# Attention and two mixtures of experts on one core: another order of the first blocks, later splits for the third unit, and other counts of idle products

## The chip, the core and the metric

The kernel runs on one core of a Trainium2 chip. A core has a matrix engine (PE, TensorE), a vector engine (DVE, VectorE), an engine for functions of one input (ACT, ScalarE), a general engine (POOL, GpSimd), and SP, which here only issues transfers. Each works through its own list of instructions and waits on semaphores for the others. The metric is the device time of one launch in microseconds, the median of several runs. Before the change it is 643.78 us (three runs, 643.44 to 646.37).

## What is computed

Attention over 2 batches of 8 heads (576 positions, head size 64), in which each query keeps only its 32 largest scores; the result, 1152 tokens of 512 numbers, goes through two mixtures of 8 experts, each token to its best expert. The change lies in the attention and in the first mixture's start:

```python
scores = scale * np.matmul(q, k.transpose(0, 1, 3, 2))
kth = np.partition(scores, -top_k, axis=-1)[..., -top_k:-top_k + 1]
scores = np.where(scores >= kth, scores, -1000000000.0)
attn = np.exp(scores - np.max(scores, axis=-1, keepdims=True))
attn = attn / (np.sum(attn, axis=-1, keepdims=True) + 1e-09)
return np.matmul(attn, v)
# then, for each mixture: expert_idx = argmax(x @ w_gate), experts' two products, gate_w
```

## The kernel before

The attention is cut into 8 units (a batch and two heads), and a unit into 9 blocks of 128 queries: four chunks for each head, and one block (the fifth) with the last 64 queries of both heads. `tiles` lists them, `seq` is the list of all 72 blocks in the order in which they are worked. Everything is in program order: the scheduler is switched off (`manual_schedule`), so each engine does its instructions in the order in which the code writes them.

One block goes through this pipe: PE makes the scores (L298) into one of two banks `sc`; ACT copies them to `s` (L301); DVE folds the 576 scores to 160 candidates (`folds`, L318 to L324, the first of them called `hi`) and takes the 32 largest (`chain`, L334 and L336, result `top`); POOL makes two limits `nb` from them (L356); ACT makes a penalty `r` (L361); POOL subtracts it (`m`, L366); ACT takes the exponential (`kept`, L370); PE turns it (L376, into `pt`) and ACT copies that out (`pT`, L381); PE multiplies by the values (L393, into `xb`), and ACT copies those out (L406). In step `i` of the loop DVE selects block `i` and, interleaved, folds block `i + 1`; the scores of block `i + 3` are asked for at the end of the step; POOL and ACT work on block `i - 1` and `i - 2`.

Queries and keys are multiplied as sums of two rounded parts. The parts are made by `split` on POOL (L231, L234), for unit 0 by `part_of` on three engines (L472, L474, L475), from the raw loads `qraw` and `kraw`; the results are `qs` and `ks`. PE turns them (`turn`, L242) through a page of PSUM that ACT copies to `qkT` (L251, for unit 0 L483 and L485, tails L256 and L257). `begin` does this for unit 0, and `jobs` is a table of which step turns, splits or loads for a later unit: `at(i, f, ...)` puts a call into step `i`.

`spin(n, o)` issues `n` products of a zero tile into a place that nobody reads (L458 in the attention, L1059 in the mixtures); `ones` and `idle` are its operands.

After the last block follows a drain (`rest`, `side`), in which the last three blocks' products are finished, then a ranking of tokens by expert, the gather of the tokens, and the experts.

Of the kernel before, what the change touches and what calls it, by code (L numbers as in the profile page):

```python
# [10 lines left out]
F32 = mybir.dt.float32  # L11
F32R = mybir.dt.float32r
BF = mybir.dt.bfloat16
# [34 lines left out]
def attn_moe_moe_kernel(ctx, tc, q, k, v, g1, w11, w12, capacity, g2, w21, w22, out):  # L48
# [13 lines left out]
    small = [ctx.enter_context(tc.tile_pool(name=f"msm{i}", bufs=1)) for i in range(2)]  # L62

    with tc.manual_schedule():
        jp = consts.tile([128, 128], I32)
        nc.gpsimd.iota(jp, pattern=[[1, 128]], base=0, channel_multiplier=-1)
        ident = consts.tile([128, 128], F32)
        nc.vector.tensor_scalar(ident, jp, 0.0, None, op0=OP.is_equal)
        identr = consts.tile([128, 128], F32R)
        nc.vector.tensor_scalar(identr, jp, 0.0, None, op0=OP.is_equal)  # L70
        negid = consts.tile([128, 128], BF)
        nc.vector.tensor_scalar(negid, jp, 0.0, -1.0, op0=OP.is_equal, op1=OP.mult)
        coef = consts.tile([128, 2], F32)
        nc.vector.memset(coef[:, 0:1], -scale)
        nc.vector.memset(coef[:, 1:2], BIG)
        before = consts.tile([128, 128], BF)
        nc.vector.tensor_scalar(before, jp, 0.0, None, op0=OP.is_gt)
        ones = consts.tile([128, 128], BF)
        nc.vector.memset(ones, 1.0)
        idle = consts.tile([128, 256], BF)  # L80
        nc.vector.memset(idle, 0.0)
    x_d = dram.tile([N + 128 - TAIL, Dm], F32, name="x")
    nov = [most_blocks(N, min(cap, N)), most_blocks(N, N)]
    LAST = NCOL - 1 + nov[0]
# [72 lines left out]
    def attention():  # L157
# [9 lines left out]
        with tc.tile_pool(name="ald", bufs=2) as ld, tc.tile_pool(name="awk", bufs=2) as wk, \  # L167
# [70 lines left out]
            def flipped(u, j, hh, c, o):  # L238
                z = st[u]
                rows_, a_ = parts[j]  # L240
                m = 128 if c < M else TAIL
                nc.tensor.transpose(o, z[rows_][:m, c, hh, a_:a_ + 2].rearrange("s a d -> s (a d)"), identr[:m, :m])  # L242
# [7 lines left out]
                    flipped(u, j, hh, c, pt[:, c * 128:(c + 1) * 128])  # L250
                pend.append(lambda: nc.scalar.activation(z["qk"][:, hh, j, :M * 128], pt.bitcast(F32), AF.Copy))  # L251

            def put_tails(u, pt):
                z = st[u]
                ptf = pt.bitcast(F32)[:, :384].rearrange("p (h j s) -> p h j s", h=2, j=3)
                nc.scalar.activation(z["qk"][:, :, 1:, M * 128:], ptf[:, :, 1:], AF.Copy)  # L256
                nc.scalar.activation(z["qtail"][:, :, :64], ptf[:, :, 0], AF.Copy)  # L257

            def turn_tails(u):
                pt = ps.tile([128, 512], F32R, name="pg")  # L260
# [43 lines left out]
            def bank():  # L304
                return ps.tile([128, 2, 512], F32, name="sc", bufs=2)
# [89 lines left out]
            def value(k):  # L395
                u, t = seq[k]
                values(u, t, pTs.pop(k))
# [58 lines left out]
            def spin(n, o):  # L456
                for _ in range(n):
                    nc.tensor.matmul(o, ones, idle, start=True, stop=True)  # L458
# [5 lines left out]
            def begin():  # L464
                z = st[0]
                z["qk"] = ld.tile([128, 2, 3, S], F32R, name="qkT")
                for nm in ("k", "q"):
                    z[nm + "s"] = ld.tile([128, NC, 2, 2 + (nm == "k"), D], F32R, name=nm + "s")

                def part_of(nm, hh, c0, c1, m):  # L470
                    t, r = z[nm + "s"][:m, c0:c1, hh], z[nm][:m, c0:c1, hh]
                    nc.scalar.activation(t[:, :, :, 0], r, AF.Copy)  # L472
                    if nm == "k":
                        nc.gpsimd.tensor_scalar(t[:, :, :, 2], r, 1.0, 1.0, op0=OP.mult, op1=OP.mult)  # L474
                    nc.vector.tensor_tensor(t[:, :, :, 1], r, t[:, :, :, 0].bitcast(F32), op=OP.subtract)  # L475

                def whole(hh, j, act):
                    pt = (ps.tile([128, 512], F32R, name="pg") if j == 0 else
                          bank().rearrange("p w k -> p (w k)").bitcast(F32R)[:, :512])
                    for c in range(M):  # L480
                        flipped(0, j, hh, c, pt[:, c * 128:(c + 1) * 128])
                    if act:
                        nc.scalar.activation(z["qk"][:, hh, j, :M * 128], pt.bitcast(F32), AF.Copy)  # L483
                    else:
                        nc.vector.tensor_copy(z["qk"][:, hh, j, :M * 128], pt.bitcast(F32))  # L485

                one, two, both = slice(0, 1), slice(1, 2), slice(0, 2)
                part_of("k", one, 0, M, 128)
                part_of("q", one, 0, M, 128)
                part_of("k", both, M, NC, TAIL)  # L490
                part_of("q", both, M, NC, TAIL)
                part_of("k", two, 0, M, 128)
                part_of("q", two, 0, M, 128)
                whole(0, 1, True)
                whole(0, 0, False)
                whole(0, 2, True)
                for hh in range(2):
                    for j in range(3):
                        g = hh * 3 + j
                        flipped(0, j, hh, M, xb.bitcast(F32R)[:, g * 64:(g + 1) * 64])  # L500
                put_tails(0, xb.bitcast(F32R))
                whole(1, 1, True)
                held = {0: scores(0, 0)}
                whole(1, 2, True)
                whole(1, 0, True)
                for i in (1, 2):
                    held[i] = scores(*seq[i])
                return held

            def v_first():  # L510
# [9 lines left out]
                v_gates(0, ps.tile([128, NC * 128], F32, name="pt"))  # L520
                flush()

            seq = [(u, t) for u in range(NU) for t in range(NT)]
            load(0, ("k",))
            load(0, ("q",), nc.scalar)
            warm = wk.tile([128, 1], F32, name="warm", bufs=1)
# [25 lines left out]
            def at(i, f, *a):  # L552
                jobs.setdefault(i, []).append((f, a))

            for u in range(NU):
                i0 = u * NT
                if u >= 1:
                    for n_ in range(6):
                        at(i0 - 10 + n_, turn, u, n_ // 3, n_ % 3)
                    at(i0 - 4, turn_tails, u)  # L560
                    at(i0 - 3, v_turn, u)
                    at(i0 - 2, v_gates, u)
                if u > 1:
                    at(i0 - 19, split, u, "q", 0)
                    at(i0 - 18, split, u, "q", 1)
                    at(i0 - 17, split, u, "k", 0, (0, 1))
                    at(i0 - 16, split, u, "k", 0, (2,))
                    at(i0 - 16, split, u, "k", 1)
                if u + 3 < NU:
                    at(i0 + 5, load, u + 3)  # L570
                at(i0 + 2, wide, 2 * u)
                at(i0 + 4, wide, 2 * u + 1)
                if u == NU - 1:
                    continue
                at(i0 + NT + 1, missed, u)
                at(i0 + NT + 3, total, u)
                at(i0 + NT + 4, logits, u)
                for d, w in enumerate(((0, 2, 128), (2, M, 128), (M, NC, TAIL))):
                    at(i0 + NT + 5 + d, normed, u, *w)
# [46 lines left out]
            z = st[u]  # L626
            rest, side = bank(), bank()
            top = z["top"][:, NT - 1, TOPK - 1:]
            value(L - 3)
            expo(L - 2, *ms.pop(L - 2))  # L630
            value_out(L - 3)
# [2 lines left out]
            f = wk.tile([128, NU, NT, 2], BF, name="f", bufs=1)  # L634
            nc.vector.tensor_scalar(f, flv, 0.0, None, op0=OP.is_ge)
            total(u)
            spin(4, rest[:, 0, :256])
            pTs[L - 2] = flipped_out(flip(L - 2))
            rs = z["rs"]
            nc.vector.reciprocal(rs, rs)  # L640
# [1 line left out]
                w, k_ = ((0, c), (1, c - 2), (0, 2))[min(c // 2, 2)]  # L642
                nc.tensor.transpose(side[:, w, k_ * 128:k_ * 128 + 128], kept[(L - 1) % 3][:, c * 128:c * 128 + 128], ident)
            counted = flags(rest[:, 1, :], f)
            spin(3, rest[:, 0, :256])
            value(L - 2)
            pT = wk.tile([128, NC, 128], F32, name="pT")
            b_ = nc.vector.tensor_copy(pT[:, 2:M], side[:, 1, :256].rearrange("p (c s) -> p c s", c=2))
# [142 lines left out]
    def moe(i, pools, src, lg, w1, w2, limit):  # L791
# [4 lines left out]
        with ExitStack():  # L796
# [28 lines left out]
            def whole(o, t):  # L825
                with nc.allow_low_precision(reason="sums with at most one term, a whole number below 256"):
                    red(o, t, axis=AX.X, op=OP.add)
# [228 lines left out]
            def spin(n):  # L1056
                o = ps.tile([128, 512], F32, name="pp", bufs=4)
                for _ in range(n):
                    nc.tensor.matmul(o[:, :256], ones, idle, start=True, stop=True)  # L1059
# [312 lines left out]
            def begin():  # L1372
                bank()
                choose(0, nch)
                count(0, nch)
                nc.scalar.activation(dl, dl, AF.Exp)
                spin(26)
                weave(*ranking())
                assign()
                weights(0, 0)  # L1380
                weights(0, 1)
                for a, (r, t, m) in enumerate(COLS):
                    if 0 < r < 3:
                        bring(a)
                first_split = splits(0, 0)
                for f in first_split[:4]:
                    f()
                xTs[0] = wk.tile([128, KD, 2, SIZES[0]], F32R, name="xT")
                for q in tiles_of(0):
                    rows_in(0, *q)  # L1390
                for f in first_split[4:]:
                    f()
                weights(1, 0)
# [211 lines left out]
```

## Time and profile before

| | |
|---|---|
| median of three runs | 643.78 us |
| the profiled execution | 644.56 us, its span 642.8 us |
| attention, first fold to last selection | 10.2 to 274 us |
| drain and ranking | 274 to about 294 us |
| the experts of both mixtures | the rest |
| busy over the span | PE 90%, DVE 79%, ACT 69%, POOL 38% |

The profile is of one execution. Times are counted from the start of the span. An engine's busy share says little by itself: the attention, the drain and the experts have different limits. What an instruction waited for is given behind it in brackets, and for DVE the waits of a stretch are summed up in a view of their own. The granted clock of PE stands as 1.00 (2.4 GHz) or 0.50 (1.2 GHz); the record of it begins at 31.7 us, and before that the view fills in 1.00, so there the durations of the products have to be read.

### The profile page before, as it was taken

The page shows a single profiled execution, that of the slowest core. Times are in us where ns is not written, and L with a number is a line of the kernel's source. Part 1 is how long each engine was busy: PE and PEld are TensorE (multiplying, and loading weights), DVE is VectorE, ACT ScalarE, POOL GpSimd, SP SyncE. Part 2 cuts the span into 40 slices and gives each one's busy share as a digit, 9 for nine tenths or more (in the row PEclk, how much of TensorE's full clock was granted, in tenths as well). Part 3 has the DMA queues.
Part 4 walks back from the last instruction along what each step waited for, and adds up shares of the span by engine and source line. Part 5 has one row for each costly group of instructions (what it writes and reads, how often), then busy time and mean ns, then how long its engine had stood idle before and what let it go on. Part 6 is the DMA issues. An engine that isn't in the chain of part 4 may idle for free. (4 is left out here: it accounts for less than half of the span.)

```text
span 642.8 us, 13274 instructions
## 1 busy us (share of the span) xinstructions
PE 580.7 (90%) x4319; PEld 531.9 (83%) x4319; DVE 507.4 (79%) x1885; ACT 446.3 (69%) x963; POOL 246.7 (38%) x427
## 2 busy tenths in 40 slices
PE   5799888888888888777999999999898999999994
PEld 4698777777777776665988999999898889999984
DVE  5799999999999999945766678872358587888740
ACT  5499888888888897723665777773144577788750
POOL 7668676767675454524020100100014311101010
PEclk9999999999999999868999999999798999999998
DMA  6693303030300000007995668877167867668660
GB/s 147 171 262 41 94 2 92 2 93 2 93 2 20 1 20 2 19 20 224 341 287 191 211 214 240 261 221 234 53 207 271 282 209 251 228 235 279 218 219 13
DMA packets 79597, 95.96 MB, mean 149 GB/s; under 512 B 33749, under 2 KB 42453, under 8 KB 79520
## 3 DMA queue, kind: packets, MB, share of 16 engines
q1 hardware_dynamic: 74624, 84.07, 43.0%
q0 software_dynamic: 3696, 10.66, 5.3%
q8 instruction: 37, 0.61, 0.4%
q10 hardware_dynamic: 1200, 0.30, 0.2%
q14 instruction: 40, 0.33, 0.2%
HBM read 82.29 MB, written 13.22 MB: 149 GB/s over the span
## 5 line engine op out<-in xcount | busy, mean ns | idle before, releaser
L366 POOL TENSOR_TENSOR m<-s,r 128x576 f32<-128x576 f32 x71 | 100.8, 1420 | 53.4 <-ACT r L361 53.2
L393 PE MATMUL xb<-vx,pT 128*128 128x73 f32 (+1 forms) x800 | 98.3, 273 | 3.6 <-ACT xl L406 2.6
L393 PEld LDWEIGHTS xb<-vx,pT 128*128 128x128 f32 (+1 forms) x800 | 89.9, 185 | 8.0 <-ACT xl L406 4.2
L946 PE MATMUL pp<-xT,w1c 128*128 128x416 f32 (+4 forms) x320 | 93.5, 361 | 0.0
L884 DVE TENSOR_TENSOR w2c<-raw,w2c 128x512 fp32r<-128x512 f32 x116 | 76.9, 684 | 19.8 <-ACT w2c L883 19.8
L883 ACT ACTIVATE w2c<-raw 128x512 fp32r<-128x512 f32 x120 | 72.0, 624 | 15.7 <-DMA raw<-in_moe_w_dram 8.8
L948 PE MATMUL pp<-xT,w1c 128*128 128x208 f32 (+4 forms) x320 | 78.2, 244 | 0.0
L884 DVE TENSOR_TENSOR w1c<-raw,w1c 128x512 fp32r<-128x512 f32 x96 | 60.7, 686 | 13.8 <-ACT w1c L883 13.1
L298 PE MATMUL sc<-qkT 128*128 128x288 f32 x256 | 53.3, 333 | 19.6 <-DVE cand L322 18.1
L985 PE MATMUL pp<-hT,w2c 128*128 128x384 f32 (+3 forms) x256 | 68.7, 350 | 0.0
L334 DVE MAX8 top<-y 128x8 f32<-128x160 f32 x216 | 66.4, 307 | 0.1
L298 PEld LDWEIGHTS sc<-qkT 128*128 128x128 f32 x256 | 38.1, 199 | 32.5 <-DVE cand L322 29.4
L301 ACT ACTIVATE s<-sc 128x576 f32<-128x576 f32 x72 | 47.0, 653 | 22.3 <-PE sc L298 19.7
L376 PE MATMUL pt<-ident,kept 128*128 128x128 f32 x355 | 55.1, 287 | 7.8 <-ACT kept L370 7.0
L987 PE MATMUL pp<-hT,w2c 128*128 128x192 f32 (+3 forms) x256 | 61.7, 241 | 0.0
L948 PEld LDWEIGHTS pp<-xT,w1c 128*128 128x128 f32 x320 | 61.2, 191 | 0.2
L946 PEld LDWEIGHTS pp<-xT,w1c 128*128 128x128 f32 x320 | 60.2, 188 | 0.8
L925 ACT ACTIVATE t<-pp 128x192 f32<-128x192 f32 (+4 forms) x112 | 34.9, 311 | 36.3 <-PE pp L948 27.9
L381 ACT ACTIVATE pT<-pt 128x640 f32<-128x640 f32 x71 | 50.2, 706 | 11.7 <-PE pt L376 10.5
L361 ACT ACTIVATE r<-s,nb 128x576 f32<-128x576 f32 x71 | 54.6, 769 | 4.0 <-POOL nb L356 4.0
L883 ACT ACTIVATE w1c<-raw 128x512 fp32r<-128x512 f32 x96 | 53.4, 619 | 5.8 <-DMA raw<-in_moe_w_dram 5.8
L370 ACT ACTIVATE kept<-m,nb 128x576 f32<-128x576 f32 x71 | 54.7, 771 | 2.4 <-POOL m L366 2.3
(301 smaller groups left out, 1424.8 us busy)
## 6 DMA issues: line engine op xcount, KB each, us to landing
raw<-in_moe_w_dram SPq DMA_DIRECT2D x62, 1024.0 KB, 5.6
out_dram<-zero SPq DMA_DIRECT2D x1, 2304.0 KB, 8.7
y<-yr POOLq DMA_DIRECT2D x8, 256.5 KB, 4.1
kraw<-in_k_dram SPq DMA_DIRECT2D x8, 256.0 KB, 3.0
vraw<-in_v_dram SPq DMA_DIRECT2D x16, 128.0 KB, 2.8
vx<-in_v_dram SPq DMA_DIRECT2D x16, 128.0 KB, 2.9
raw<-in_moe_w_dram SPq DMA_DIRECT2D x4, 512.0 KB, 4.5
x<-xn SPq DMA_DIRECT2D x15, 128.0 KB, 2.0
```

The costliest lines, as they stand in the source:

```text
L298: nc.tensor.matmul(sc[:, w, :W2], l, r[:, w * W2:(w + 1) * W2], start=(n_ == 0), stop=(n_ == len(ops) - 1))
L334: ops.append(lambda w=w, cur=cur: nc.vector.max(w, cur))
L366: nc.gpsimd.tensor_tensor(m, s, r, op=OP.subtract)
L370: nc.scalar.activation(kept[k % 3][:, :S], m, AF.Exp, bias=nb[:, 0:1], scale=scale)
L376: nc.tensor.transpose(pt[:, o], kept[k % 3][:, o], ident)
L393: nc.tensor.matmul(o, pT[:, c2, cols], z["v"][:, c2, hh], start=(c2 == 0), stop=(c2 == NC - 1))
L883: nc.scalar.activation(o[:, 0], src_, AF.Copy)
L884: eng.tensor_tensor(o[:, 1], src_, o[:, 0].bitcast(F32), op=OP.subtract)
L946: nc.tensor.matmul(ph[:, :2 * n].rearrange("p (w n) -> p w n", w=2), w[f][:, 0, d], xT[:, d, :, :n], start=st, stop=False)
L948: nc.tensor.matmul(ph[:, :n], w[f][:, 1, d], xT[:, d, 0, :n], start=False, stop=sp)
L985: nc.tensor.matmul(py[:, :2 * n].rearrange("p (w n) -> p w n", w=2), w[f][:, 0, o], hT[:, f, :, :n], start=st, stop=False)
L987: nc.tensor.matmul(py[:, :n], w[f][:, 1, o], hT[:, f, 0, :n], start=False, stop=sp)
```

## The change

Eight edits, all of them moves or counts. (1) The operands of the idle products are set first on DVE, and 17 idle products go ahead of everything else on PE. (2) `begin` makes the parts of head 1 after head 0 is turned, not before. (3) The second block is chunk 1 of head 0, not chunk 0 of head 1 (in unit 0 the blocks with `t` 1 and 2 change places), so its scores follow at once; head 1 is turned after both, in pages `pt` and `pg` in place of the score banks, and `qtail` is copied later. (4) The turns of unit 1 start one step later, so its last one and `turn_tails` share step 5. (5) The splits of unit 2 go from steps -1, 0, 1, 2, 2 to steps 3, 4, 5, 6, 6. (6) 7 idle products go ahead of the values of the third last block in the drain. (7) The two later groups there have 2 and 6 in place of 4 and 3. (8) The ranking's group has 18 in place of 26.

```diff
     with tc.manual_schedule():
+        ones = consts.tile([128, 128], BF)
+        nc.vector.memset(ones, 1.0)
+        idle = consts.tile([128, 256], BF)
+        nc.vector.memset(idle, 0.0)
         jp = consts.tile([128, 128], I32)
...
                 part_of("k", both, M, NC, TAIL)
                 part_of("q", both, M, NC, TAIL)
-                part_of("k", two, 0, M, 128)
-                part_of("q", two, 0, M, 128)
-                whole(0, 1, True)
-                whole(0, 0, False)
-                whole(0, 2, True)
+                whole(0, 1, wide_page())
+                whole(0, 0, page(), False)
+                whole(0, 2, wide_page())
...
-                put_tails(0, xb.bitcast(F32R))
-                whole(1, 1, True)
+                tails = put_tails(0, xb.bitcast(F32R), True)
+                part_of("k", two, 0, M, 128)
                 held = {0: scores(0, 0)}
-                whole(1, 2, True)
-                whole(1, 0, True)
-                for i in (1, 2):
-                    held[i] = scores(*seq[i])
+                part_of("q", two, 0, M, 128)
+                held[1] = scores(*seq[1])
+                tails()
+                whole(1, 1, spare())
+                whole(1, 2, page())
+                whole(1, 0, spare())
+                held[2] = scores(*seq[2])
                 return held
...
-            seq = [(u, t) for u in range(NU) for t in range(NT)]
+            seq = [(u, t) for u in range(NU) for t in [0] + ([2, 1] if u == 0 else [1, 2]) + list(range(3, NT))]
+            spin(17, xb[:, :256])
             load(0, ("k",))
...
-                        at(i0 - 10 + n_, turn, u, n_ // 3, n_ % 3)
+                        at(i0 - (9 if u == 1 else 10) + n_, turn, u, n_ // 3, n_ % 3)
...
-                    at(i0 - 19, split, u, "q", 0)
-                    at(i0 - 18, split, u, "q", 1)
-                    at(i0 - 17, split, u, "k", 0, (0, 1))
-                    at(i0 - 16, split, u, "k", 0, (2,))
-                    at(i0 - 16, split, u, "k", 1)
+                    i1 = i0 - (15 if u == 2 else 19)
+                    at(i1, split, u, "q", 0)
+                    at(i1 + 1, split, u, "q", 1)
+                    at(i1 + 2, split, u, "k", 0, (0, 1))
+                    at(i1 + 3, split, u, "k", 0, (2,))
+                    at(i1 + 3, split, u, "k", 1)
...
             top = z["top"][:, NT - 1, TOPK - 1:]
+            spin(7, rest[:, 0, :256])
             value(L - 3)
...
-            spin(4, rest[:, 0, :256])
+            spin(2, rest[:, 0, :256])
             pTs[L - 2] = flipped_out(flip(L - 2))
...
             counted = flags(rest[:, 1, :], f)
-            spin(3, rest[:, 0, :256])
+            spin(6, rest[:, 0, :256])
             value(L - 2)
...
                 nc.scalar.activation(dl, dl, AF.Exp)
-                spin(26)
+                spin(18)
```

What stands on ACT in the opening, between the parts of the tails and the third block's scores, before (`ks` and `qs` are the parts, `qkT` the turned ones, `s` the scores):

```order
L472 ACTIVATE qs<-qraw 64x2x64
L472 ACTIVATE ks<-kraw 128x4x64
L472 ACTIVATE qs<-qraw 128x4x64
L483 ACTIVATE qkT<-sc 128x512 x2
L256 ACTIVATE qkT<-xb 128x2x2x64
L257 ACTIVATE qtail_116<-xb 128x2x64
L483 ACTIVATE qkT<-sc 128x512
L301 ACTIVATE s<-sc 128x576
L483 ACTIVATE qkT<-sc 128x512
L483 ACTIVATE qkT<-pg 128x512
L301 ACTIVATE s<-sc 128x576 x2
```

and on ACT in the changed kernel (its lines are numbered some five higher):

```order
L477 ACTIVATE qs<-qraw 64x2x64
L486 ACTIVATE qkT<-sc 128x512 x2
L256 ACTIVATE qkT<-xb 128x2x2x64
L477 ACTIVATE ks<-kraw 128x4x64
L306 ACTIVATE s<-sc 128x576
L477 ACTIVATE qs<-qraw 128x4x64
L306 ACTIVATE s<-sc 128x576
L259 ACTIVATE qtail_116<-xb 128x2x64
L486 ACTIVATE qkT<-pt 128x512
L486 ACTIVATE qkT<-pg 128x512
L486 ACTIVATE qkT<-pt 128x512
```

The two rounded parts of head 1 (128x4x64) moved from ahead of head 0's copies to either side of the first scores, and the second scores moved ahead of head 1's three copies.

What stands on POOL from the end of the opening to the second pair of limits, before (`nb` are the limits of a block, `qs` and `ks` from 128x8x64 are splits of unit 2):

```order
L546 MEMSET zero 128x513
L234 TENSOR_SCALAR qs<-qraw 128x8x64
L231 TENSOR_TENSOR qs<-qraw,qs 128x8x64
L234 TENSOR_SCALAR qs<-qraw 64x2x64
L231 TENSOR_TENSOR qs<-qraw,qs 64x2x64
L356 TENSOR_TENSOR nb<-top,coef 128x2
L234 TENSOR_SCALAR ks<-kraw 128x8x64
L231 TENSOR_TENSOR ks<-kraw,ks 128x8x64
L124 MEMSET lg_90 128x80
L125 MEMSET lg_91 128x160
L126 MEMSET revm_102 128x160
L127 MEMSET code_104 128x40
```

and on POOL in the changed kernel:

```order
L560 MEMSET zero 128x513
L361 TENSOR_TENSOR nb<-top,coef 128x2
L124 MEMSET lg_90 128x80
L125 MEMSET lg_91 128x160
L126 MEMSET revm_102 128x160
L127 MEMSET code_104 128x40
L371 TENSOR_TENSOR m<-s,r 128x576
L361 TENSOR_TENSOR nb<-top,coef 128x2
```

The first block's limits now follow the opening's last fill directly, and no split stands between them and the first subtraction `m`.

## Rows read from the trace of the kernel before

**Rows 1.** Summed waits of DVE, 0 to 265 us (total, times, longest).

```profile
DVE hi L318 <- ACT s L301: 6.5, 4, 2.6
```

**Rows 2.** Stretches of 10 us: length, then busy time of each engine, PEclk, DMA share, GB/s.

```profile
50.00:60.00 10.00, 9.73 (x76) 8.54 (x76) 10.00 (x48) 9.54 (x19) 9.13 (x17) 1.00 0.37 34
```

**Rows 3.** Timeline of the opening: start us, us, engine, line, operation, [idle before <-releaser].

```profile
5.03 0.75 PE L242 MATMUL sc<-identr,ks 128*128 128x128 f32 x4 [5.03 <-DVE ks L475]
...
6.34 0.40 ACT L472 ACTIVATE qs<-qraw 128x256 fp32r<-128x256 f32 x1
...
7.23 0.44 PE L242 MATMUL xb<-identr,ks 64*128 64x64 f32 x2
...
8.15 1.29 PE L298 MATMUL sc<-qkT 128*128 128x288 f32 x4
...
9.47 0.65 ACT L301 ACTIVATE s<-sc 128x576 f32<-128x576 f32 x1 [0.49 <-PE sc L298]
...
10.16 0.31 DVE L318 TENSOR_TENSOR hi<-sc,s 128x144 f32<-128x144 f32 x1 [2.30 <-ACT s L301]
...
13.20 0.31 DVE L318 TENSOR_TENSOR hi<-sc,s 128x144 f32<-128x144 f32 x1 [0.89 <-ACT s L301]
```

**Rows 4.** Timeline of the first blocks, 16 to 31 us.

```profile
16.57 0.31 DVE L334 MAX8 top<-y 128x8 f32<-128x160 f32 x1
...
20.36 0.62 POOL L234 TENSOR_SCALAR qs<-qraw 128x512 fp32r<-128x512 f32 x1 [4.24 <-DVE cand L324]
...
21.73 2.28 PE L284 MATMUL pt<-wgh,vT 128*128 128x16 f32 x10
...
23.10 0.18 POOL L356 TENSOR_TENSOR nb<-top,coef 128x2 f32<-128x2 f32 x1
...
23.32 0.78 ACT L361 ACTIVATE r<-s,nb 128x576 f32<-128x576 f32 x1 [4.00 <-POOL nb L356]
...
24.66 0.31 DVE L318 TENSOR_TENSOR hi<-sc,s 128x144 f32<-128x144 f32 x1 [0.63 <-ACT s L301]
...
25.70 1.40 POOL L366 TENSOR_TENSOR m<-s,r 128x576 f32<-128x576 f32 x1
...
27.13 0.77 ACT L370 ACTIVATE kept<-m,nb 128x576 f32<-128x576 f32 x1 [1.89 <-POOL m L366]
...
30.97 0.31 DVE L318 TENSOR_TENSOR hi<-sc,s 128x144 f32<-128x144 f32 x1 [2.63 <-ACT s L301]
```

**Rows 5.** Timeline of two later blocks.

```profile
32.71 0.77 PE L298 MATMUL sc<-qkT 128*128 128x288 f32 x4
...
43.13 0.68 ACT L301 ACTIVATE s<-sc 128x576 f32<-128x576 f32 x1
...
45.30 0.29 DVE L318 TENSOR_TENSOR hi<-sc,s 128x144 f32<-128x144 f32 x1
```

**Rows 6.** Stretches of one clock in the drain and the ranking, columns as in Rows 2.

```profile
270.68:274.10 3.42, 1.88 (x15) 1.65 (x15) 3.07 (x14) 3.38 (x6) 1.64 (x3) 1.00 0.00 0
274.10:280.92 6.82, 6.69 (x32) 6.29 (x33) 2.10 (x7) 2.40 (x6) 1.06 (x3) 0.50 0.01 2
...
284.34:291.16 6.82, 5.21 (x35) 3.88 (x36) 5.46 (x30) 0.65 (x4) 0.46 (x2) 0.50 0.23 62
```

**Rows 7.** Timeline of PE and DVE in the drain and the ranking.

```profile
271.49 1.34 PE L393 MATMUL xb<-vx,pT 128*128 128x73 f32 x10 [1.02 <-ACT xl L406]
...
274.23 2.41 PE L393 MATMUL xb<-vx,pT 128*128 128x73 f32 x10 [0.85 <-ACT pT L381]
...
280.18 2.71 PE L393 MATMUL xb<-vx,pT 128*128 128x73 f32 x20
...
286.46 5.30 PE L1059 MATMUL pp<-idle,ones 128*128 128x256 bf16 x26
...
290.46 0.30 DVE L1150 TENSOR_TENSOR r<-isa,code 128x280 bf16<-128x280 bf16 x1
...
291.59 0.21 PE L1165 MATMUL pi<-r,onehot 128*128 128x28 bf16 x1
```

More of the change, by code (lines that the diff above doesn't have):

```diff
@@ L77, in attn_moe_moe_kernel @@
         nc.vector.tensor_scalar(before, jp, 0.0, None, op0=OP.is_gt)
[L78 to L81, printed above, removed]
     x_d = dram.tile([N + 128 - TAIL, Dm], F32, name="x")
@@ L251, in turn, with put_tails @@
                 pend.append(lambda: nc.scalar.activation(z["qk"][:, hh, j, :M * 128], pt.bitcast(F32), AF.Copy))
-            def put_tails(u, pt):
+            def put_tails(u, pt, apart=False):
                 z = st[u]
@@ L256, in put_tails, with queries @@
                 nc.scalar.activation(z["qk"][:, :, 1:, M * 128:], ptf[:, :, 1:], AF.Copy)
-                nc.scalar.activation(z["qtail"][:, :, :64], ptf[:, :, 0], AF.Copy)
+                def queries():
+                    nc.scalar.activation(z["qtail"][:, :, :64], ptf[:, :, 0], AF.Copy)
+                if apart:
+                    return queries
+                queries()
             def turn_tails(u):
@@ L475, in part_of, with whole, page, wide_page @@
                     nc.vector.tensor_tensor(t[:, :, :, 1], r, t[:, :, :, 0].bitcast(F32), op=OP.subtract)
-                def whole(hh, j, act):
-                    pt = (ps.tile([128, 512], F32R, name="pg") if j == 0 else
-                          bank().rearrange("p w k -> p (w k)").bitcast(F32R)[:, :512])
+                def whole(hh, j, o, act=True):
                     for c in range(M):
-                        flipped(0, j, hh, c, pt[:, c * 128:(c + 1) * 128])
+                        flipped(0, j, hh, c, o[:, c * 128:(c + 1) * 128])
                     if act:
-                        nc.scalar.activation(z["qk"][:, hh, j, :M * 128], pt.bitcast(F32), AF.Copy)
+                        nc.scalar.activation(z["qk"][:, hh, j, :M * 128], o.bitcast(F32), AF.Copy)
                     else:
-                        nc.vector.tensor_copy(z["qk"][:, hh, j, :M * 128], pt.bitcast(F32))
+                        nc.vector.tensor_copy(z["qk"][:, hh, j, :M * 128], o.bitcast(F32))
+                def page():
+                    return ps.tile([128, 512], F32R, name="pg")
+                def wide_page():
+                    return bank().rearrange("p w k -> p (w k)").bitcast(F32R)[:, :512]
+                def spare():
+                    return ps.tile([128, NC * 128], F32, name="pt").bitcast(F32R)[:, :512]
                 one, two, both = slice(0, 1), slice(1, 2), slice(0, 2)
```

## The prediction

> **What bounds the kernel now.** I read the stretches of 10 us first. From 31 to 274 us DVE is busy without a gap: 10.00 of 10.00 us in a stretch like [rows 2]. There the attention is as fast as DVE's selections, one step of the block loop in 3.58 us (from the fold at 30.97 to the one at 45.30 are four steps, [rows 4, 5]). Nothing in that part of the change takes work from DVE, so the attention gets shorter only where DVE waits. The view of DVE's waits says where: its first fold of a block waited for ACT's copy of the scores four times, 6.5 us in all [rows 1]. The timeline shows the four: 2.30 at 10.16 and 0.89 at 13.20 [rows 3], 0.63 at 24.66 and 2.63 at 30.97 [rows 4]. The last two have one cause. The first block's 32 largest were done at 16.88, but its limits `nb` came at 23.10, because POOL had the splits of unit 2 ahead of them and stood 4.24 us for their data, until 20.36. ACT stood 4.00 us for `nb`; `kept` of block 0 then started at 27.13, PE turned it and only behind that made the sixth block's scores, and DVE folded those at 30.97 [rows 4].
>
> After 274 us the bound is PE: 6.69 us busy of 6.82, at clock 0.50, with ten value products in 2.41 us where the same ten took 1.34 at clock 1.00 [rows 6, 7]. Then the ranking: DVE's table `r` is done at 290.76, but the products that use it start at 291.59, behind 26 idle products (5.30 us) [rows 7].
>
> **The opening.** PE has nothing to do before 5.03 [rows 3]. The operands of the idle products now are set first on DVE, before anything that waits for POOL, so 17 of them can run early; at 5.30/26 = 0.204 us each [rows 7] they take 3.5 us. If they begin by 1.5 us, which I take, they end ahead of the first turn and cost nothing; if they began at 2.0 they would cost 0.5. What they give is the clock. Before 31.7 us the clock column is no record, but four score products took 1.29 us at 8.15 and 0.77 at 32.71 [rows 3, 5]: the opening ran at the lower level (1.2 GHz).
>
> With the clock still low, the first scores start when the copied tails are there, at 8.15 as now (the moved parts of head 1 make ACT earlier, but PE's tails end at 7.67 either way [rows 3]); they are copied at 9.47. But in the new order ACT makes the queries' part of head 1 behind that copy (0.40, [rows 3]) and DVE its remainder, which stands ahead of the first fold in DVE's list; so the first fold comes at 10.9, 0.7 later than now. With the clock high, the scores take 0.5 less and the tails end earlier, by an estimate of 0.35 (the last 0.44 of them halves, and the turns ahead run into a wait for DVE's remainders): first fold at 10.0.
>
> That order of waits is a place where the Trainium skill ("TensorE: Matmul & The Clock Gate", on engine queue depths in its section on the array) speaks against the change: it says that ACT, DVE and POOL take their lists strictly in order. The trace agrees, with `nb` at 23.10 behind a split though its input was ready at 16.88 [rows 4]. If DVE could pass the waiting instruction, the first fold would stand at 9.2 in place of 10.0 and the sum below would be some 0.7 better, 638.8.
>
> The folds of block 0 take 13.20 - 0.89 - 10.16 = 2.15. Block 1's scores (head 0, already turned) follow the first directly, so the wait of 0.89 goes. The first selection starts at 13.05 (low clock) or 12.15 (high), against 13.20. The third block's scores need three turns and three copies of head 1, some 3.5 us after the first two, and DVE wants them 3.58 us later: they are hidden, with about 1 us left.
>
> `nb` of block 0 now follows POOL's last fill, so at about 17. Then `kept` of block 0 is held by the next thing: ACT's copy of the gate logits, behind the gate products (2.28 us from 21.73, [rows 4]), which stand behind the fifth block's scores, which wait for DVE to free a bank. That chain moves with DVE, by 0.15 (low) or 1.05 (high). With some 0.3 for the copy it ends at 24.0 - 0.15 + 0.3 = 24.15 or at 23.25. From `kept` to the sixth block's fold are 30.97 - 27.13 = 3.84: fold at 28.0 or 27.1. DVE is ready four steps after its first selection, 27.4 or 26.5, so 0.6 us of waiting stays and the gain is 3.0 or 3.9.
>
> Something goes back behind it. The splits of unit 2 now lie in steps 3 to 6. The queries' took POOL 23.10 - 20.36 = 2.74 us, the keys', with three parts to their two, by that at most 4.1; with `m` and `nb` (1.40 and 0.18, [rows 4]) four times POOL has 13.2 us to do there, and some fills, in 14.3 us of steps. So `m` may come late by part of a split; I put up to 0.9. Step 5 has a turn and the tails in one page, so PE stands for ACT's copy between them, and ACT has one copy more (about the 0.65 of a score copy, [rows 3]). Now the scores of a block are there early there: copied by 43.81, folded at 45.30, 1.5 us of cover [rows 5]. The two together use that up. I put 0.5 us on it and on the next block's scores, which PE may still make at the low clock. If the cover held all, the cost would be nothing; if POOL's lateness added up over the steps, 2 us. Opening: 3.4 us with the high clock, 2.5 without.
>
> **The drain.** The hole on PE before the values at 274.23 is 0.85 us [rows 7]. In the stretch that ended at 274.10, PE was busy 1.88 of 3.42 us, and then the clock fell for 6.82 us [rows 6]. Seven idle products at the high clock (half of 0.204 each) take 0.7 and fit into the hole. Two bounds. If the clock stays low all the same, they take 1.4 and push the values back by 0.6; the next group saves 2 x 0.2, the third adds 3 x 0.2: 0.8 us lost in all. If the clock stays high, the 6.69 us of PE work shrink by half, less some 0.4 in which PE then waits for ACT's copies: 2.9 us won. The record gives no ground to choose between them; I take 1.0 won, the middle.
>
> **The ranking.** 18 idle products from 286.46 end at 290.1 at the low clock. The first product that uses `r` then starts at about 290.85, not 291.59: 0.74 won. At the high clock 26 would have ended before `r` too, and nothing is won. The clock was low there [rows 6], behind a stretch without PE work, which stays: I take 0.6. Moves that cost nothing: the two settings on DVE (in its wait for POOL's table), head 1's pages, and `qtail`, not read before the fifth block.
>
> **Sum.** 3.4 + 1.0 + 0.6 = 5.0. The profiled execution took 644.56 us (span 642.8), 0.78 over the median of 643.78; from it comes 639.6, from the median 638.8. Since part of that 0.78 may be the low clock in the drain, whose gain I have counted, I stay near the first: 639.5. The experts start from the ranking, their first weights and gathers wait for its tables, so what is won before them stays won.
>
> **Rivals.** (a) The idle products don't do what they are there for: the clock stays low in the opening and in the drain. For it: in the opening turns follow them, and the turns at 5.03 and 7.23 and the scores at 8.15 stayed low [rows 3]. Then 2.5 - 0.8 + 0.7 = 2.4 won: 641.4 from the median, 642.2 from the profiled execution; 642. (b) The drain runs wholly at the high clock: 3.4 + 2.9 + 0.6 = 6.9, so 637.3. For it: the hole they fill lies just ahead of the fall; against it: three blocks without score products come before, in which the clock already fell once. (c) Slower: POOL. If `m` waits out every split in steps 3 to 6, it is late by 2.74 + 4.1 = 6.8 us in all; over the cover of 1.5 that is 5.3 lost on DVE, against 3.9 won before it. With the drain at its bad bound 0.8 more is lost, and the ranking may give nothing: 2.2 slower, 646.0. It decides as soon as scores come over 1.5 us late. For it: those four steps leave POOL hardly a gap. Against it: the splits of later units lie in steps of the same kind, and DVE's stretch there is full [rows 2].
>
> **Chances and range.** The forecast 0.50, (a) 0.25, (b) 0.17, (c) 0.08. What a measurement can tell from no change is about 0.5%: under 640.6 counts as faster, over 647.0 as slower. Of the forecast's own spread (638 to 641) three quarters lie under 640.6, with (b) and a little of (a): 0.56 faster. Of (c) half might go past 647: 0.05 with what I haven't seen. Same: 0.39. Range: the good end is (b) with an opening 1 us better, 636.3; the bad end is (a) with 0.6 more lost in steps 3 to 8, 642.6.
>
> **What would show it.** Right: four score products near 0.8 us at about 8 us; the first fold at 10.0 and no wait of DVE at the second block; `nb` at about 17; the sixth block's fold at 27 to 28 behind a wait of 0.6; DVE's last selection 3 to 4 us earlier; the ranking's first product right behind `r`. Wrong: score products of 1.3 us in the opening, a DVE wait of over 1 us between 30 and 50 us (POOL's splits then), ten value products of 2.4 us in the drain, or experts that take longer by what came before them.

## The result and the profile after

The changed kernel takes 635.70 us (median of four runs, 632.82 to 635.93) against 643.61 beside it (643.28 to 646.37): a ratio of 0.986, with an interval of 0.982 to 0.990. The profiled executions took 635.8 (span 634.0) and 644.56 (span 642.8), so 8.8 us went between the two traces. The forecast was 639.5 with a range of 636.3 to 642.6: the right side, but the gain is nearly twice as large, and it does not lie where I put it.

DVE's waits for the scores, 0 to 265 us, are the first row to look at (total, times, longest). Before it was 6.5 us in four waits [rows 1].

```profile
DVE hi L323 <- ACT s L306: 4.8, 4, 2.5
```

Still four waits, and only 1.7 us less. The timeline of the opening in the changed kernel (start, us, engine, line, operation, idle before) answers to [rows 3, 4]:

```profile
1.32 3.79 PE L463 MATMUL xb<-idle,ones 128*128 128x256 bf16 x17 [1.32 <-DVE idle L68]
...
7.26 1.51 PE L303 MATMUL sc<-qkT 128*128 128x288 f32 x8
...
9.61 0.30 DVE L323 TENSOR_TENSOR hi<-sc,s 128x144 f32<-128x144 f32 x1
...
11.68 0.29 DVE L323 TENSOR_TENSOR hi<-sc,s 128x144 f32<-128x144 f32 x1
...
16.12 0.18 POOL L361 TENSOR_TENSOR nb<-top,coef 128x2 f32<-128x2 f32 x1
...
22.70 0.77 ACT L375 ACTIVATE kept<-m,nb 128x576 f32<-128x576 f32 x1
...
26.53 0.31 DVE L323 TENSOR_TENSOR hi<-sc,s 128x144 f32<-128x144 f32 x1 [0.47 <-ACT s L306]
```

That is the opening as forecast, a little better: eight score products in 1.51 us (the high clock), the first fold at 9.61, the second block without a wait, the limits `nb` at 16.12, the sixth block's fold at 26.53 against 30.97, 4.44 us earlier [rows 4]. By the eleventh block all of it has gone back. The timeline of step 5 and what follows, where the row of before has a fold at 45.30 without a wait [rows 5]:

```profile
38.69 0.25 PE L242 MATMUL pg<-identr,qs 64*128 64x64 f32 x1 [1.28 <-ACT qkT L251]
...
39.40 2.41 PE L398 MATMUL xb<-vx,pT 128*128 128x73 f32 x10
...
42.53 1.31 PE L303 MATMUL sc<-qkT 128*128 128x288 f32 x4
...
44.55 0.31 DVE L323 TENSOR_TENSOR hi<-sc,s 128x144 f32<-128x144 f32 x1 [2.47 <-ACT s L306]
...
49.08 0.31 DVE L323 TENSOR_TENSOR hi<-sc,s 128x144 f32<-128x144 f32 x1 [0.85 <-ACT s L306]
```

Two waits of DVE, 3.32 us, follow products that take nearly twice as long (ten value products 2.41 us, where [rows 7] has them at 1.34 and 2.41). The stretches by clock (length, busy time of PE, PEld, DVE, ACT, POOL, then PEclk, DMA share, GB/s) say why:

```profile
12.07:32.55 20.48, 17.47 (x84) 16.46 (x82) 19.03 (x91) 11.94 (x21) 13.34 (x43) 0.50 0.70 171
32.55:39.37 6.82, 5.42 (x46) 4.86 (x45) 6.82 (x35) 6.25 (x13) 6.50 (x16) 1.00 1.03 328
39.37:46.20 6.83, 6.83 (x37) 6.46 (x37) 4.36 (x21) 4.36 (x10) 2.55 (x12) 0.50 1.03 193
...
274.00:281.72 7.72, 5.49 (x49) 5.26 (x49) 4.32 (x19) 2.74 (x7) 2.98 (x12) 1.00 0.00 1
281.72:291.96 10.24, 8.84 (x65) 6.60 (x66) 7.80 (x41) 1.72 (x5) 1.47 (x3) 0.50 0.41 134
```

PE stood 1.28 us for the page `pg` in step 5, and at 39.37 the granted clock fell to 0.50 for 6.83 us. The fold of the eleventh block, at 49.08, stands 0.20 later than before, and from there to the last selection (274.14 against 273.86) the attention of the two traces differs by 0.2 to 0.3 us. The drain, though, kept the high clock. Its timeline and that of the ranking answer to [rows 7]:

```profile
272.06 0.93 PE L463 MATMUL sc<-idle,ones 128*128 128x256 bf16 x7
...
273.94 1.34 PE L398 MATMUL xb<-vx,pT 128*128 128x73 f32 x10 [0.95 <-ACT pT L386]
...
277.14 2.35 PE L398 MATMUL xb<-vx,pT 128*128 128x73 f32 x20
...
279.92 0.49 DVE L690 SCALAR_TENSOR_TENSOR lg<-xb,rs,lg 128x8 f32<-128x8 f32 x2
...
283.31 4.03 PE L1075 MATMUL pp<-idle,ones 128*128 128x256 bf16 x18
...
287.31 0.30 DVE L1166 TENSOR_TENSOR r<-isa,code 128x280 bf16<-128x280 bf16 x1
287.66 0.21 PE L1181 MATMUL pi<-r,onehot 128*128 128x28 bf16 x1 [0.32 <-DVE r L1166]
```

The last gate logits (`lg`) stood at 283.32 before: 3.40 us won up to there, 3.7 in the drain alone (from the last selection to `lg` 9.46 us before, 5.78 after). The ranking's first product stands right behind `r`: 3.93 won. By PE's last product before a jump between the two mixtures (453.23 before, 448.64 after) it is 4.6: the low clock after the ranking lasts 3.41 us in place of 6.83. The other half of the gain comes where nothing was changed, between the two mixtures. PE there before (its first 16 products after the jump, and the first `key` of the second ranking on DVE):

```profile
452.09 1.14 PE L939 MATMUL pp<-xT,raw 128*128 128x128 f32 x8
...
455.83 3.75 PE L939 MATMUL pp<-xT,raw 128*128 128x128 f32 x16 [2.60 <-PEq L1209]
...
461.30 0.17 DVE L1421 SCALAR_TENSOR_TENSOR key<-pi,rev 128x8 f32<-128x8 f32 x1 [6.27 <-PE pi L1122]
```

and after:

```profile
447.50 1.14 PE L955 MATMUL pp<-xT,raw 128*128 128x128 f32 x8
...
449.28 2.05 PE L955 MATMUL pp<-xT,raw 128*128 128x128 f32 x16 [0.63 <-ACTq L1225]
...
452.29 0.17 DVE L1437 SCALAR_TENSOR_TENSOR key<-pi,rev 128x8 f32<-128x8 f32 x1 [1.85 <-PE pi L1138]
```

PEq and ACTq in these rows stand for the sequencers of PE and ACT. Before, PE stood 2.60 us for its own sequencer, at the jump over a loop that is skipped (`spill`), and the clock then fell for 6.83 us (455.00 to 461.83); after, it stood 0.63, put down to ACT's sequencer, and the clock stayed. The products stand 4.6 us earlier ahead of it and the `key` 9.0 behind it: 4.4 us won, 2.0 of them the wait.

### The profile page after: what moved, and what is told of

It reads as the page before. It is cut to its first block, busy times and chain, and to the rows that moved or that the text cites. A ratio compares the mean times of both kernels' runs of the same rounds, so it can differ in the third digit from the quotient of the medians.

```text
span 634.0 us, 13305 instructions
## 1 busy us (share of the span) xinstructions
PE 579.5 (91%) x4336; PEld 529.3 (83%) x4336; DVE 508.4 (80%) x1885; ACT 446.0 (70%) x963; POOL 247.2 (39%) x427
## 5 line engine op out<-in xcount | busy, mean ns | idle before, releaser
L339 DVE MAX8 top<-y 128x8 f32<-128x160 f32 x216 | 71.7, 332 | 0.1
```

The lines of the kernel that those rows point to most:

```text
L339: ops.append(lambda w=w, cur=cur: nc.vector.max(w, cur))
```

## The experiments

All eight kernels compute the whole result. Times beside them are of the kernel before on the same chip: 644.82 us for the first four, 643.39 for the others.

**e1_pad: only the place of PE's code.** The kernel before, with 17 idle products of 8 columns at the head of PE's list (34 more PE instructions, a weight load and a product each), their operands set first on DVE as in the change (that part of the edit is left out here):

```diff
+            for _ in range(17):
+                nc.tensor.matmul(xb[:, :8], ones, idle[:, :8], start=True, stop=True)
             load(0, ("k",))
```

> The kernel before, with 17 idle products of only 8 columns as the first work of PE (and their operands set first on DVE). They put 34 instructions into PE's list, as many as the changed kernel has more there up to the second mixture, and end before PE's first turn at 5.0 us. Theory of PE's code position: between the two mixtures PE stood 2.60 us for its own sequencer before and 0.63 after, because the jump over the skipped loop falls elsewhere in PE's code; so this kernel stands about 0.6 us there, and the clock does not fall behind it: 639.3 (643.7 less 2.0 and 2.4). Rival, that the wait or the clock there follows from the earlier start of everything behind the drain: no change, 643.7, and 2.6 us of waiting.

Measured: 640.05 us (six runs), ratio 0.993 (0.990 to 0.996). PE's waits, 440 to 465 us:

```profile
PE pp L941 <- ACTq L1211: 0.6, 1, 0.6
```

0.6 in place of 2.6, and no fall of the clock there: from PE's last product before the jump (450.86) to the `key` (454.51) it is 4.4 us shorter than before, as in the changed kernel. Products 447 us earlier in the program take the stall away, so it depends on where the code lies. The opening was not better for it (DVE waited 7.6 us for scores).

**e2_drain: drain and ranking alone** (6, 7, 8), on the kernel before.

```diff
+            spin(7, rest[:, 0, :256])
-            spin(4, rest[:, 0, :256])
+            spin(2, rest[:, 0, :256])
-            spin(3, rest[:, 0, :256])
+            spin(6, rest[:, 0, :256])
-                spin(26)
+                spin(18)
```

> The kernel before, with only the changed counts of idle products in the drain (7, 2, 6) and the ranking (18); PE's code up to the second mixture is as long as before. Theory that these counts made the drain's gain: the drain runs at the high clock, the last logits come 3.4 to 3.7 us earlier, the gather 3.9 to 4.4 us; total 639.0 to 639.8, with the 2.60 us wait of PE between the mixtures as before. Rival, that the clock in the drain was high by where the opening left it: the drain stays low, 644 to 645. Rival on the wait between the mixtures (earlier start does it): 635.

Measured: 640.08 us (eight runs), ratio 0.992 (0.989 to 0.996). The groups add up to as many instructions as before, and the wait is there again, with the clock low for 3.4 us behind it:

```profile
PE pp L940 <- PEq L1210: 2.3, 1, 2.3
```

The drain kept the high clock to 283.25; from the last selection (275.73) to the logits (281.52) it is 3.7 us shorter than before.

**e3_open: the opening alone.** The changed kernel with e2's edit undone (4, 3 and 26).

> The changed kernel with the drain's and the ranking's idle products as before (4, 3, 26, none ahead of the values). Theory: the new opening is 4 us ahead at the sixth block and gives it all back at blocks 9 and 10, where the clock is low from 39.4 us; the last fold stands 0.2 us later than before, the drain runs low as before. What is left is PE's shorter wait between the mixtures (code position): 639 to 640. Rival, that opening and drain share the clock's phase: drain high, 636.

Measured: 637.74 us (four runs), ratio 0.990 (0.987 to 0.993). DVE's waits for scores 4.7 us, PE's wait between the mixtures 0.8: the place of e1. The clock fell at 39.45 for 6.83 us as in the changed kernel, and the last fold stands 0.39 later than before. That the drain would run low as before did not come: it was at the low clock for 3.41 us (274.96 to 278.38), and from the last selection to the logits it took 7.34 us with the old counts, against 9.46 before. That fits a time below the 639 to 640 expected.

**e4_turns_back: part (4) undone.** Unit 1's turns start a step earlier again, the last one no longer shares step 5 with the tails.

```diff
-                        at(i0 - (9 if u == 1 else 10) + n_, turn, u, n_ // 3, n_ % 3)
+                        at(i0 - 10 + n_, turn, u, n_ // 3, n_ % 3)
```

> The changed kernel with the turns of unit 1 one step earlier, as before, so that step 5 holds no turn beside the tails. Theory: PE's 1.28 us wait for the page in step 5 made the clock fall at 39.4 us; without it the clock stays high, the waits of 2.47 and 0.85 us at blocks 9 and 10 go, the last fold comes about 3.3 us earlier, 632.4. Rival, that POOL's splits in steps 3 to 6 make the blocks late: the waits at blocks 9 and 10 stay, 635.7.

Measured: 632.35 us (four runs), ratio 0.982 (0.979 to 0.985). The stretches, same columns as above, from the rise of the clock here, cut where the clock of the changed kernel turned:

```profile
32.42:39.37 6.95, 6.83 (x57) 6.26 (x57) 6.95 (x34) 6.47 (x13) 6.43 (x16) 1.00 1.03 363
39.37:46.20 6.83, 6.61 (x62) 5.94 (x61) 6.83 (x33) 6.47 (x16) 5.20 (x15) 1.00 1.08 186
```

and DVE's waits:

```profile
DVE hi L323 <- ACT s L306: 1.4, 2, 1.0
```

No fall, DVE full, and from the seventh block on the folds stay 3.2 to 3.3 us ahead of before. The splits of unit 2 are still in steps 3 to 6 here, so POOL was not what took the gain.

**e5_256: e4 with 222 more PE instructions,** 256 more than before in all: 78 products of 8 columns at the start in place of 17 of 256, and 78 of 64 in place of 28 of 256 in the group behind the ranking's table.

```diff
-            spin(17, xb[:, :256])
+            for _ in range(78):
+                nc.tensor.matmul(xb[:, :8], ones, idle[:, :8], start=True, stop=True)
...
-                    spin(28)
+                    for _ in range(78):
+                        nc.tensor.matmul(o[:, :64], ones, idle[:, :64], start=True, stop=True)
```

> The kernel with the turns of unit 1 back, whose PE list is made 222 instructions longer before the second mixture (78 idle products of 8 columns in place of 17 of 256 at the start, 78 of 64 columns in place of 28 of 256 behind the ranking), so 256 instructions (16 KB of code, the size of one code load of PE in the record) longer than the kernel before. Theory that PE's position in blocks of its code decides: the wait for PE's sequencer between the mixtures is back at 2.3 to 2.6 us. Rival, that any longer list or the early start of PE does it: 0.6 to 0.8 us, as in the four kernels that have 34 more. The opening's clock stays low in this kernel, so its total (634 to 639) says little; the wait is what is looked at.

Measured: 636.21 us in one run. The wait is back:

```profile
PE pp L956 <- PEq L1228: 2.9, 1, 2.9
```

So it is not "more is better"; that the effect repeats after 256 instructions rests on this one run.

The run shows something else. Its 78 small products did not bring the high clock early: the first eight score products took 2.35 us, and the record of the clock begins with 1.00 at 33.33. What the new order gives at the low clock can be read from it:

```profile
7.66 2.35 PE L303 MATMUL sc<-qkT 128*128 128x288 f32 x8
...
27.28 0.31 DVE L323 TENSOR_TENSOR hi<-sc,s 128x144 f32<-128x144 f32 x1 [0.40 <-ACT s L306]
```

The sixth block's fold is 3.69 us ahead of before, the last one 2.51; in e4, with the high clock at first, it is 4.37 and 3.25. So the order brings most of the lead, and the clock from the 17 idle products some 0.7.

**e6_fill5: the changed kernel with the hole of step 5 (the 1.28 us in which PE stood) filled,** so that the page is waited for as long, but by a busy PE.

```diff
+            def fill5():
+                for _ in range(24):
+                    nc.tensor.matmul(xb[:, 440:504], ones, idle[:, :64], start=True, stop=True)
...
+                    if u == 1:
+                        at(i0 - 4, fill5)
                     at(i0 - 4, turn_tails, u)
...
```

> The changed kernel with 24 idle products of 64 columns (in free columns of the page of values) between the last turn and the tails in step 5, where PE stood 1.28 us for the page. The wait for the page stays, PE is only busy in it. Theory that PE's standing there made the clock fall: the clock stays high past 39 us, the waits at blocks 9 and 10 go, 632.5 as with the turns back. Rival, that the wait itself (turn, copy, tails in one page) makes the blocks late: waits at blocks 9 and 10 stay about 3 us, 635.7.

Measured: 633.37 us (four runs), ratio 0.986 (0.982 to 0.989); by it alone not to be told from the changed kernel's 0.986, which was timed on another occasion. The trace is clearer. Timeline of step 5:

```profile
37.69 0.86 PE L568 MATMUL xb<-idle,ones 128*128 128x64 bf16 x24 [0.24 <-ACT xl L411]
...
38.72 0.24 PE L242 MATMUL pg<-identr,qs 64*128 64x64 f32 x1 [0.17 <-ACT qkT L251]
...
39.42 1.34 PE L398 MATMUL xb<-vx,pT 128*128 128x73 f32 x10
...
42.86 0.31 DVE L323 TENSOR_TENSOR hi<-sc,s 128x144 f32<-128x144 f32 x1 [0.72 <-ACT s L306]
```

The tails start at 38.72 as without the filling (38.69), but the clock does not fall, the value products take 1.34 in place of 2.41, and the waits of 2.47 and 0.85 become one of 0.72. Behind it the folds are 2.44 us ahead of before. Against e4's 3.28 at the same block, the page itself costs some 0.8; against the 0.20 late of the changed kernel, the clock costs 2.64. In both traces with the open hole (the changed kernel and e3) the clock fell there, in none of the five without it (e4 to e8).

**e7_nodrain: e4 without the drain's products** (none, 4 and 3; the ranking keeps 18).

> The kernel with the turns of unit 1 back, with the drain's idle products as before the change (none ahead of the values, 4, 3), the ranking's 18 kept. Theory that the drain's products keep the clock up: a fall at 271 to 275 us, the last logits 1.5 to 3.6 us later than with them, 634.5. Rival, that the clock there only follows the place of its steps in time (a kernel with the old counts had it high): no change, 632.4.

Measured: 638.31 us (twelve runs, 635.52 to 642.75), ratio 0.993 (0.991 to 0.996), so 6 us over e4; but it has 16 PE instructions fewer than e4, and the wait between the mixtures is back (waits of PE, then the drain's products):

```profile
PE pp L954 <- PEq L1224: 2.4, 1, 2.4
```

```profile
270.46 1.96 PE L398 MATMUL xb<-vx,pT 128*128 128x73 f32 x10 [1.72 <-ACT pT L386]
...
275.21 2.44 PE L398 MATMUL xb<-vx,pT 128*128 128x73 f32 x20
```

Against e4 (1.34 for the ten, the twenty at 273.62) the drain is 1.6 to 1.7 us longer: the clock fell at 270.99, for 3.41 us. The two profiled executions are 4.6 us apart: at the end of PE's products ahead of the jump only 0.25 of the drain's loss is left, and the stall and the low clock of 6.83 us behind it make 4.3 (4.4 between before and after). I had not counted the shift of the code, so the expected 634.5 missed.

**e8_fill02: e4 with three more holes of PE filled,** ten idle products of 256 columns ahead of the scores asked for in steps 0 and 1 and ahead of the first flip.

```diff
+                if i < 2:
+                    spin(10, xb[:, :256])
                 if i + 3 < L:
...
+                if i == 2:
+                    spin(10, xb[:, :256])
                 if i >= 2:
```

> The kernel with the turns of unit 1 back, and 10 idle products each in PE's three holes of steps 0 to 2 (ahead of the scores of blocks 3 and 4 and of the first turned exponentials), where the clock is low from 12 to 32 us. Theory that the low clock there costs DVE's waits of 0.47 and 0.98 us at blocks 5 and 6: the clock stays high from 5 us on, both waits shrink, 631.2 (1.2 less). Rival, that the idle products stand in front of work at the low clock (10 of them 2.1 us): the waits grow, 633 to 635.

Measured: 631.95 us (six runs), ratio 0.983 (0.981 to 0.986). The stretch that ran low in the changed kernel:

```profile
12.07:32.55 20.48, 17.88 (x143) 15.64 (x144) 20.48 (x98) 15.12 (x28) 16.25 (x47) 1.00 0.67 164
```

DVE is busy for 20.48 of 20.48 us (19.03 in the changed kernel) and waits for no scores from there to the end of the attention; its folds are 4.23 us ahead of before, though the first one came at 10.37, since the clock rose only at 10.73 here, not at 5 us as expected. As the rise itself came later, this run does not tell apart whether the filled holes or the later rise kept the clock up; that the wait of 0.98 at the seventh block goes with the low clock, it shows. With e4 it is the fastest of the ten kernels; between the two the intervals do not decide.

## Why the prediction missed

**The opening: mechanism right, the repayment mis-sized.** Each row up to 31 us came out as written, a little earlier; the copy of the first scores was done at 8.93, and the fold still waited for the remainder of head 1 ahead of it in DVE's list and came at 9.61, as I had assumed. The high clock itself held only from 5.24 to 12.07, and by e5 it brought 0.7 of the lead, where my two cases (3.0 and 3.9) stood 0.9 apart. What failed is the sentence on step 5: "The two together use that up. I put 0.5 us on it". By the traces step 5 cost 3.5 us: 3.30 ahead at the ninth block became 0.20 behind at the eleventh. I asked only whether the scores would be late by more than their cover, 1.5 us at the high clock. I wrote that PE stands for ACT's copy there, but did not ask what the clock does behind such a hole: PE stands 1.28 us, and the clock falls. e6 shows that this is the cause: the same page, a filled hole, no fall, 2.64 us back. The page itself is the other 0.8 (e4 against e6). From 4.44 to 3.37 the lead had fallen at the seventh block, by a wait of 0.98 in the low stretch up to 32.55, which goes when the clock is high there (e8). My rival (c), and my sign of being wrong ("a DVE wait of over 1 us between 30 and 50 us (POOL's splits then)"), had the place but the wrong engine: with the same splits in the same steps, e4 has no wait of DVE after 31.3 us.

The net of the opening is somewhat better than these two traces say. Before 31.7 us the clock of the kernel before left no record, but e1 and e2, which keep its opening, have their rise at 36.04 and 37.49 and end the attention 1.3 and 1.9 us later than its profiled execution. So that one was an early case, and against the others the new opening gains some 1.1 to 1.6 us.

**The drain: between my bounds I took the middle, and it was beyond the good end.** Forecast 1.0, bounds -0.8 and 2.9; 3.7 in the changed kernel and in e2. The clock stayed high to 281.72, which rival (b) asked for. How much is the products' own doing is less clear. From the last selection to the logits, five of the six kernels with the new counts take 5.8 us (the changed kernel, e2, e4, e5, e8) and e6 6.52; with the old counts it is 6.55 in e1, 7.34 in e3, 7.43 in e7 and 9.46 before. So against the three others the new counts gain 0.8 to 1.7, and the other 2 to 3 of the 3.7 are the case that the profiled execution of before fell into. The clock is part of that case: e1, without the new counts, had the high clock from 271.56 to 285.21 as well, after a fall at 268.14; and in e6, with them, the clock fell at 264.59, before they come. The clock differs there between kernels that have the same code in that stretch.

**The ranking: right.** Forecast 0.6; 0.5 by the two traces, from 3.40 at the logits to 3.93 at the first product.

**The experts: a missing term, and the largest.** "what is won before them stays won" put them at nothing, and no row behind the ranking was read for it. It is the largest error on the side on which the time left the range: without these 5.1 us the forecast would have been too low, not too high. They gave 0.7 at their start and 4.4 between the mixtures, more than half of the 8.8. The cause of the 4.4 is shown as far as this: the stall follows from how many instructions stand ahead of the jump on PE. With 0, 0, 18 and 256 more than before it lasts 2.6, 2.3, 2.4 and 2.9 us (before, e2, e7, e5); with 34 (the changed kernel, e1, e3, e4), 82 (e6) and 94 (e8) it lasts 0.6 to 0.8. In the four long cases the clock fell in the stall or behind it, for 3.41 or 6.83 us; in none of the other six did it. No edit of the change has to do with it other than by its number of instructions, and the 17 idle products at the start brought 34.

**Sum.** By the traces: opening -0.3, drain 3.7, ranking 0.5, experts' start 0.7, between the mixtures 4.4: 9.0, of which 0.2 is lost again towards the end. The forecast had 3.4, 1.0, 0.6, 0 and 0. So the opening came 3.7 short, and the drain and the experts 7.8 over; that the forecast was off by only 3.8 us is in part luck, as the two errors have opposite signs.

## What to carry to other kernels

When a move puts two users of one page into one step, price the hole it makes on PE by what the clock does behind it, not by whether its neighbours have cover: here some 0.8 us of page became 3.5 us. Idle products in such a hole are cheap to try (0.86 us of them gave 2.64 back). And any edit that changes the number of instructions on an engine can move a stall at a jump far behind it: look at the waits of an engine for its own sequencer in both traces before a gain is put down to the edit, and keep the count equal when single edits are compared.

## What was not expected of the hardware

The stall at PE's jump. In all four kernels where it is long, one transfer of 16,384 bytes of the queue that the trace calls instruction starts within 0.35 us of the end of PE's last product before the jump, and PE goes on 2.5 to 2.9 us after it started (before: started at 453.29, PE done at 453.23, on again at 455.83). Where 34 instructions were added, such a transfer started 1.7 to 2.5 us before PE was done (after: 446.13, PE done at 448.64), and the stall is short. That reads as code that is fetched too late for the jump. In e6 and e8 a transfer starts at the same place as in the four (446.75 with PE done at 447.04; 444.26 with 444.23), and PE waits 0.6 us all the same. But there the transfer before it started 8.2 us before PE was done (438.85 and 436.00), and in the four long cases 17.9 to 18.6 us before (before: 435.25). So in all ten kernels the stall is short where such a transfer started 1.7 to 8.2 us ahead of PE's end, and long where none started between 0.4 and 17 us ahead. That the code behind the jump comes with that transfer would explain it; the trace doesn't say what a transfer holds, so this is not shown.

The clock's falls are not a matter of the code alone: with the same opening it fell back to the low level at 8.16 us in e7 and at 11.94 in e4, and the kernel before, e1 and e2 rose at or before 31.7, at 36.04 and at 37.49. What a hole costs by the clock is therefore not fixed by the code: a forecast should carry both cases.
